# Eight later attention units: transposing in VectorE blocks of 32 and a ScalarE exchange in place of TensorE transposes

## The chip, the cores and the metric

The kernel runs on one core of one Trainium2 chip. The time is the device time of one execution in microseconds (us); lower is better. The kernel before took 783.46 us as the median of three runs (781.99 to 783.51). Engines are named as the profile names them: PE is TensorE, DVE is VectorE, ACT is ScalarE, POOL is GpSimd, SP issues most DMAs.

## The reference

Chunked attention is followed by a gated two-layer product. q, k and v have 8 batches, 8 heads, 576 positions and 64 dimensions; positions attend only within chunks of 64.

```
scores = scale * q_c @ k_c.T              # 64 x 64 for each batch, head and chunk
attn = exp(scores - rowmax) / (rowsum + 1e-9)
x = (attn @ v_c) laid out as 4608 x 512
h = x @ w_in                              # 512 x 2048
g = h * clip(h + 3, 0, 6) / 6
out = g @ w_out                           # 2048 x 512
```

All is float32. The kernel writes the output transposed.

## The kernel before

The 4608 tokens are nine blocks of 512. Each block has two attention units (`n`, `dp`), named "50" for block 5, first half; a unit covers four heads of the block's eight chunks, so 32 score squares of 64 x 64, which fill 128 partitions and two PSUM banks. There are 18 units. Block 0 is multiplied plainly, and the blocks 1 to 8 are taken in four pairs by a scheme of seven block products in place of eight; pair s has a first product (steps `f1` to `f7` for eight parts p) and a second (steps `s{s}.0` to `s{s}.55`). A step is six PE matmuls of 128 x 512: three passes (L354 to L356), since each operand is split into a high and a low part. The splitting is ACT's and DVE's work (L541, L544, L983, L987). Between the two products stand the sums of the scheme (L876), the relu (L761, ACT) and the gate (L764, DVE). In a first product the sums read and free PSUM banks that later steps of the same product need: `u2` and `u4` (L876, DVE, tiles u<-h,p and u<-acc,u), then the third sum (h<-acc,u), the relu, the gate.

An attention unit goes through these steps: `scores` (PE, L246) into the two-bank PSUM tile `two`; `max` (DVE, L253); `less` (DVE, L257), which subtracts the row maximum and writes the SBUF tile `e`; `exp` (ACT, L260); `sum` (DVE, L264 to L266); `share` (DVE, L284), which multiplies by the reciprocal sum; `turn` (PE, L296), eight transposes of 128 x 128 against the identity into a new `two`; `turned` (ACT, L300), which copies the transposed tile back over `e`; `product` with v (PE, L322), which in most units has the next unit's `scores` behind it as one step; and `keep` (ACT, L335). Units in the list `ROWS` ("30", "31", "40", "41") replace less, exp and sum: `negate` (DVE, L270) makes the bias, 16 exponentials of 128 x 64 with row sums (ACT, L276, two to a step) read `two` and write `e`, and `invert` (DVE, L280 and L281) ends it.

The order on every engine is made before the program is written: `Schedule.order` plays all steps through with the costs that stand in the code (1.07 us for `turn`, 1.15 us for two row exponentials and so on), due times and a fixed list of dependences, and each engine's queue gets its instructions in the order that comes out. An engine runs its queue in order, so a wait holds up all that is behind it.

The units "50" to "81" are the later ones: the order is 50, 60, 61, 51 in the stage of the second pair and 70, 80, 81, 71 in that of the third. 50, 60, 70 and 80 are prepared mostly beside a first product, the other four beside a second.

Of the kernel before, what the change touches and what calls it, by code (L numbers as in the profile page):

```python
# [9 lines left out]
F32 = mybir.dt.float32  # L10
# [8 lines left out]
P = 128  # L19
CH = 64  # L20
B, H, S, D = 8, 8, 576, 64
NDP = H // 4
NB = 8
NT = NB * CH
# [13 lines left out]
ORDER_B = (1, 5, 6, 7, 2, 4, 3)  # L38
SLOTS = 7 * NFP
HALF = [slice(0, CH), slice(CH, P)]  # L40
WARM = 12
FILL = (2.0, 4.0)
LAG = 2
ROWS = ["30", "31", "40", "41"]
XDVE = ["x0.s0c", "x0.s2", "x0.s2b", "x0.s3", "x0.s3b"]
SHARED = 0.6
OVERLAP = {"DVE": 0.07, "ACT": 0.0}
# [15 lines left out]
STEPS = SECOND - PART * 7 * (NFP - NPL)  # L63
COMBS = []
LATE = (5, 9)


class Schedule:
# [69 lines left out]
def tile_kernel(ctx: ExitStack, tc: tile.TileContext, qk_in, v_in, weights, out):  # L138
    nc = tc.nc
    PE, ACT, DVE, POOL = nc.tensor, nc.scalar, nc.vector, nc.gpsimd  # L140
# [3 lines left out]
    ap = pool("ap", 1)  # L144
# [78 lines left out]
    class Attention:  # L223


        def __init__(self, n, dp, psum=None, out=None):
            self.n, self.dp = n, dp
            self.psum = psum or (lambda: two_banks(ps_a))
            self.out = out or self.psum

        def load_qk(self, qk=None):

# [7 lines left out]

        def scores(self):
            self.s = self.psum().rearrange("p a (c t) -> p a c t", t=CH)
            for c in range(NB):
                for a, rows in enumerate(HALF):
                    for o in HALF:
                        PE.matmul(self.s[o, a, c, :], lhsT=self.qk[rows, 0, c, o], rhs=self.qk[rows, 1, c, o], start=True, stop=True)  # L246
# [6 lines left out]
            DVE.tensor_reduce(out=self.m, in_=self.flat(self.s), axis=AX.X, op=ALU.max)  # L253

        def lessen(self, e=None):
            self.e = e if e is not None else ap.tile([P, 2, NB, CH], F32, name="e")
            DVE.tensor_tensor(out=self.flat(self.e), in0=self.flat(self.s), in1=self.wide(self.m), op=ALU.subtract)  # L257

        def exp(self):
# [11 lines left out]

        def exps(self, k, e=None):
            if k == 0:
                self.e = e if e is not None else ap.tile([P, 2, NB, CH], F32, name="e")
            for c in range(2 * k, 2 * k + 2):
                ACT.activation(out=self.flat(self.e)[:, c], in_=self.flat(self.s)[:, c], func=AF.Exp, bias=self.m[:, c:c + 1], scale=SCALE,  # L276
                               accum_out=self.z[:, c:c + 1])
# [20 lines left out]
        def turned(self, part=(0, 1)):  # L298
            of = slice(part[0], part[-1] + 1)
            ACT.copy(out=self.aT[:, of], in_=self.tp[:, of])  # L300

        def transpose(self):
            self.turn()
# [324 lines left out]
    def attention(u, due, scores=(), less=(), keep=(), bank=None):  # L628
        n, dp = int(u[0]), int(u[1])
        a = heads[u]  # L630
# [4 lines left out]
            heads[after].scores()  # L635

        e = spare.get("e" + u, lambda: None)
        rows = [("less", "DVE", 1.23, lambda: a.lessen(e()), less), ("exp", "ACT", 1.06, a.exp, ()), ("sum", "DVE", 1.68, a.total, ())]
        if u in ROWS:
            rows = [("negate", "DVE", 0.12, a.negate, ()), *[(f"exp{k}_", "ACT", 1.15, lambda k=k: a.exps(k, e() if k == 0 else None), less if k == 0 else ()) for k in range(8)],  # L640
                    ("invert", "DVE", 0.45, a.invert, ())]
        steps = [("scores", "PE", 1.30, a.scores, ["qk" + u, *scores]), ("max", "DVE", 1.23, a.largest, ()), *rows, ("share", "DVE", 1.22, a.share, ()), ("turn", "PE", 1.07, a.turn, ()),
                 ("turned", "ACT", 1.02, a.turned, ()), ("product", "PE", 2.26 if after else 1.50, products if after else a.product,
                  ["v" + u, *(["qk" + after, *[x for _ in HALF for x in work.take(*RINGS[bank], "product" + u, [made[u], *alike.get(u, [])])]] if after else [])]),
                 ("keep", "ACT", 1.24 if after else 1.03, a.keep, keep)]
        if n == 0:
# [184 lines left out]
    def swap():  # L831
        nonlocal op, tp
        std.close()
        op = pool("op2", 2)
        tp = pool("tp", 2)
# [294 lines left out]
```

## Time and profile before

| what | value |
| --- | --- |
| median of three runs | 783.46 us |
| profiled execution, device time | 782.89 us |
| its span (first to last instruction) | 781.1 us |
| PE busy | 772.8 us, 99% |
| DVE busy | 644.8 us, 83% |
| ACT busy | 398.2 us, 51% |
| POOL busy | 70.7 us, 9% |
| PE share of the chain that ended last | 94% |
| granted TensorE clock | 0.999 |

The chain that ended last is followed back from the last instruction; what stands on it set the end. Busy shares are averages over stages with different limits. A PE matmul's shown duration is longer than the time until the next can start, since matmuls are pipelined.

### The profile page before, as it was taken

The numbers are of one execution on the slowest core, as the hardware profiler recorded it, in microseconds if no ns is written. First come the engines' busy times: TensorE is split into PE (matmuls) and PEld (weight loads), VectorE is DVE, ScalarE is ACT, GpSimd is POOL, SyncE is SP. The second block draws the span as 40 slices with busy tenths as digits, with TensorE's granted clock in tenths as the row PEclk, the third lists the DMA queues.
The fourth block names the chain that finished last, engine by engine and source line by source line (L and its number), as shares of the span: only waits on it lengthen the run. The fifth ranks groups of instructions, "written<-read, shape, count | busy, mean of one in ns | idle before, by whom it ended". The sixth has DMA issues, their size and how long they took to land.

```text
span 781.1 us, 14021 instructions
## 1 busy us (share of the span) xinstructions
PE 772.8 (99%) x5604; PEld 635.3 (81%) x5604; DVE 644.8 (83%) x808; ACT 398.2 (51%) x593; POOL 70.7 (9%) x55
## 2 busy tenths in 40 slices
PE   8999999999999999999999999999999999999998
PEld 4788888887888888888888878888888888888887
DVE  6999999999999999867998677678997657679741
ACT  4999843566667744344744434436644333355330
POOL 0000000000000001323200003231100013222000
PEclk9999999999999999999999999999999999999999
DMA  9999999878869997566667685667557665566572
GB/s 371 405 402 328 341 350 308 297 242 251 265 214 337 345 349 246 192 215 229 220 236 256 223 283 189 217 227 242 204 193 222 216 204 194 197 210 202 194 238 90
DMA packets 69426, 198.06 MB, mean 254 GB/s; under 512 B 7024, under 2 KB 19568, under 8 KB 65008
## 3 DMA queue, kind: packets, MB, share of 16 engines
q1 hardware_dynamic: 69216, 197.03, 73.7%
q8 instruction: 44, 0.72, 0.4%
q14 instruction: 22, 0.18, 0.1%
q10 hardware_dynamic: 144, 0.13, 0.0%
HBM read 153.09 MB, written 44.04 MB: 252 GB/s over the span
## 4 chain that ended last, share of the span: by engine, by line
PE 94%; DVE 3%; DMA 1%; issue 0%; SPq 0%; ACT 0%; DVEq 0%; ACTq 0%
PE acc L354 21%; PE acc L355 21%; PE acc L356 21%; PE h L354 8%; PE h L356 8%; PE h L355 8%; PE two L246 2%; PE two L296 2%; PE h L322 2%; DMA out_t<-u 1%; DMA b<-hl 1%; PE h L172 1%; PE two L322 1%; DVE wb L764 0%; PE h L370 0%
## 5 line engine op out<-in xcount | busy, mean ns | idle before, releaser
L354 PE MATMUL acc<-wa,ws 128*128 128x512 f32 (+1 forms) x536 | 209.4, 391 | 0.3 <-DVE u L876 0.3
L356 PE MATMUL acc<-wa,ws 128*128 128x512 f32 (+1 forms) x536 | 207.8, 388 | 0.0
L355 PE MATMUL acc<-wa,ws 128*128 128x512 f32 (+1 forms) x536 | 207.8, 388 | 0.0
L983 ACT CAST wa<-wb 128x1024 fp32r<-128x1024 f32 x96 | 100.4, 1052 | 93.4 <-PE acc L356 53.6
L987 DVE TENSOR_TENSOR wa<-wb,wa 128x1024 fp32r<-128x1024 f32 x96 | 122.6, 1289 | 21.3 <-ACT wa L983 21.2
L354 PEld LDWEIGHTS acc<-wa,ws 128*128 128x128 f32 x536 | 100.7, 188 | 21.7 <-DVE u L876 0.8
L356 PEld LDWEIGHTS acc<-wa,ws 128*128 128x128 f32 x536 | 100.6, 188 | 20.7
L355 PEld LDWEIGHTS acc<-wa,ws 128*128 128x128 f32 x536 | 100.7, 188 | 19.9
L950 POOL TENSOR_TENSOR wb<-wb 128x512 f32<-128x512 f32 x24 | 32.9, 1372 | 634.6 <-DVE wb L764 321.4
L761 ACT ACTIVATE r<-acc,half 128x512 f32<-128x512 f32 x90 | 61.3, 687 | 42.3 <-DVE acc L876 37.5
L761 ACT ACTIVATE r<-h,half 128x512 f32<-128x512 f32 x38 | 26.2, 689 | 103.0 <-DVE h L876 95.8
L764 DVE SCALAR_TENSOR_TENSOR wb<-r,acc 128x512 f32<-128x512 f32 x90 | 60.8, 681 | 5.3 <-ACT r L761 5.0
L355 PE MATMUL h<-wa,ws 128*128 128x512 f32 (+1 forms) x144 | 55.2, 383 | 0.0
L356 PE MATMUL h<-wa,ws 128*128 128x512 f32 (+1 forms) x144 | 55.2, 383 | 0.0
L354 PE MATMUL h<-wa,ws 128*128 128x512 f32 (+1 forms) x144 | 55.2, 383 | 0.0
L876 DVE TENSOR_TENSOR u<-h,p 128x512 f32<-128x512 f32 x32 | 21.9, 686 | 30.1 <-PE h L356 24.5
L876 DVE TENSOR_TENSOR acc<-acc,u 128x512 f32<-128x512 f32 x48 | 33.0, 695 | 8.6 <-PE acc L356 8.5
L952 POOL TENSOR_TENSOR g<-wb,wb 128x512 f32<-128x512 f32 x24 | 37.0, 1542 | 1.9
L764 DVE SCALAR_TENSOR_TENSOR wb<-r,h 128x512 f32<-128x512 f32 x38 | 25.8, 679 | 11.6 <-ACT r L761 11.6
L354 PE MATMUL acc<-wa,wa 128*128 128x512 f32 x88 | 34.9, 396 | 0.0
L355 PE MATMUL acc<-wa,wa 128*128 128x512 f32 x88 | 34.3, 390 | 0.0
L356 PE MATMUL acc<-wa,wa 128*128 128x512 f32 x88 | 34.3, 390 | 0.0
(199 smaller groups left out, 1391.8 us busy)
## 6 DMA issues: line engine op xcount, KB each, us to landing
ws<-b SPq DMA_DIRECT2D x84, 512.0 KB, 4.6
ws<-a SPq DMA_DIRECT2D x72, 512.0 KB, 4.5
qk<-qk_in SPq DMA_DIRECT2D x17, 1024.0 KB, 7.8
wa<-b SPq DMA_DIRECT2D x28, 512.0 KB, 6.2
a<-wa SPq DMA_DIRECT2D x40, 256.0 KB, 6.0
v<-v_in SPq DMA_DIRECT2D x17, 512.0 KB, 5.7
wa<-w_in_out SPq DMA_DIRECT2D x8, 1024.0 KB, 12.5
wb<-w_in_out SPq DMA_DIRECT2D x8, 1024.0 KB, 10.9
```

Source lines behind the costliest of these rows:

```text
L246: PE.matmul(self.s[o, a, c, :], lhsT=self.qk[rows, 0, c, o], rhs=self.qk[rows, 1, c, o], start=True, stop=True)
L322: PE.matmul(po[s][o, a, i, :], lhsT=self.v[rows, a, i, o], rhs=self.aT[rows, a, i, o], start=True, stop=True)
L354: PE.matmul(ps, lhsT=a_h, rhs=b_h, start=first, stop=False, skip_group_check=more)
L355: PE.matmul(ps, lhsT=a_h, rhs=b_l, start=False, stop=False, skip_group_check=more)
L356: PE.matmul(ps, lhsT=a_l, rhs=b_h, start=False, stop=last, skip_group_check=more)
L761: ACT.activation(out=t["r"], in_=ps(), func=AF.Relu, bias=half, scale=1.0 / 6.0)
L764: work.add("gate" + name, "DVE", 0.69, ["relu" + name, *more], lambda: DVE.scalar_tensor_tensor(out=out(), in0=t["r"], scalar=1.0, in1=ps( ...
L876: return lambda: DVE.tensor_tensor(out=out(), in0=x(), in1=y(), op=ALU.add)
L950: work.add(id_("t1."), "POOL", 1.45, [id_("gate3."), id_("gate2.")], lambda f=gq: POOL.tensor_tensor(out=f(0, 1), in0=f(0, 1), in1=f(0, 0) ...
L952: work.add(id_("t2."), "POOL", 1.45, [id_("t1."), id_("gate7.")], lambda f=gq, p=p: POOL.tensor_tensor(out=t2_of(p), in0=f(1, 1), in1=f(0, ...
L983: ACT.copy(out=g_ops[s, i, pp][:, :, 0], in_=src())
L987: work.add(low, *(("POOL", 2.5) if on else ("DVE", 1.22)), [high], lambda i=i, pp=pp, src=src, on=POOL if on else DVE: on.tensor_tensor(ou ...
```

## The change

For the units 50, 51, 60, 61, 70, 71, 80 and 81 (`FLIPPED`) the PE transposes and the ACT copy after them go. In their place DVE transposes the whole tile from PSUM into SBUF in blocks of 32 x 32 (`flip`), and ACT puts the blocks in their places in three steps of five copies (`swap`): `save` copies half of the blocks into the first bank of the unit's score tile in PSUM, `down` moves blocks between partition quarters in SBUF (two copies of 32 partitions), `up` moves the saved ones back (two copies). So that this exchange gives the wanted layout, `scores` writes the 64 x 64 squares to other places. Softmax of these units is done in place in PSUM: `less`, `exp`, `sum` and `share` read and write `two` instead of `e`, and `e` is first written by `flip`. Four of the units (60, 61, 80, 81) join `ROWS`; their 16 row exponentials read and write `two` in place. The planner's cost of a pair of row exponentials goes from 1.15 to 0.62 us for all units that have them, and `flip`, `save`, `down` and `up` get costs of their own.

```diff
-ROWS = ["30", "31", "40", "41"]
+ROWS = ["30", "31", "40", "41", "60", "61", "80", "81"]
+FLIPPED = ("50", "51", "60", "61", "70", "71", "80", "81")
...
         def scores(self):
             self.s = self.psum().rearrange("p a (c t) -> p a c t", t=CH)
+            if self.flipped:
+                for i in range(NB // 2):
+                    for k, o in enumerate(HALF):
+                        for a, rows in enumerate(HALF):
+                            for s, to in enumerate(HALF):
+                                PE.matmul(self.s[to, a, 2 * i + k, :], lhsT=self.qk[rows, 0, 2 * i + s, o], rhs=self.qk[rows, 1, 2 * i + s, o], start=True, stop=True)
+                return
...
-            self.e = e if e is not None else ap.tile([P, 2, NB, CH], F32, name="e")
+            self.e = self.s if self.flipped else e if e is not None else ap.tile([P, 2, NB, CH], F32, name="e")
...
+        def flip(self):
+            t = ap.tile([P, 2 * NB * CH], F32, name="e")
+            DVE.transpose(out=t, in_=self.e.rearrange("p a c t -> p (a c t)"))
+            self.aT = t.rearrange("p (a i t) -> p a i t", a=2, t=P)
+            blocks = t.rearrange("p (n h t) -> p n h t", h=2, t=CH // 2)
+            spare_ = self.e.rearrange("p a c t -> p (a c t)")[:, :NT].rearrange("p (n t) -> p n t", t=CH // 2)
+            self.moves = [[(spare_, blocks[:, :, 0])],
+                          [(blocks[hi, :, 0], blocks[lo, :, 1]) for lo, hi in QUARTER],
+                          [(blocks[lo, :, 1], spare_[hi]) for lo, hi in QUARTER]]
+
+        def swap(self, k):
+            for to, of in self.moves[k]:
+                ACT.copy(out=to, in_=of)
...
-        rows = [("less", "DVE", 1.23, lambda: a.lessen(e()), less), ("exp", "ACT", 1.06, a.exp, ()), ("sum", "DVE", 1.68, a.total, ())]
+        rows = [("less", "DVE", 1.23, lambda: a.lessen(e()), () if u in FLIPPED else less), ("exp", "ACT", 1.06, a.exp, ()), ("sum", "DVE", 1.68, a.total, ())]
         if u in ROWS:
-            rows = [("negate", "DVE", 0.12, a.negate, ()), *[(f"exp{k}_", "ACT", 1.15, lambda k=k: a.exps(k, e() if k == 0 else None), less if k == 0 else ()) for k in range(8)],
+            rows = [("negate", "DVE", 0.12, a.negate, ()), *[(f"exp{k}_", "ACT", 0.62, lambda k=k: a.exps(k, e() if k == 0 else None), less if k == 0 and u not in FLIPPED else ()) for k in range(8)],
                     ("invert", "DVE", 0.45, a.invert, ())]
-        steps = [("scores", "PE", 1.30, a.scores, ["qk" + u, *scores]), ("max", "DVE", 1.23, a.largest, ()), *rows, ("share", "DVE", 1.22, a.share, ()), ("turn", "PE", 1.07, a.turn, ()),
-                 ("turned", "ACT", 1.02, a.turned, ()), ("product", "PE", 2.26 if after else 1.50, products if after else a.product,
+        steps = [("scores", "PE", 1.30, a.scores, ["qk" + u, *scores]), ("max", "DVE", 1.23, a.largest, ()), *rows, ("share", "DVE", 1.22, a.share, ()), *([("flip", "DVE", 1.22, a.flip, less), ("save", "ACT", 0.56, lambda: a.swap(0), ()), ("down", "ACT", 1.0, lambda: a.swap(1), ()), ("up", "ACT", 1.0, lambda: a.swap(2), ())]
+                   if u in FLIPPED else [("turn", "PE", 1.07, a.turn, ()), ("turned", "ACT", 1.02, a.turned, ())]), ("product", "PE", 2.26 if after else 1.50, products if after else a.product,
```

On PE, in the first product beside which unit 50 is prepared; `wa` is a step's left operand, and lines are numbered as in each kernel (L354 before is L378 after). Before:

```order
L354 MATMUL acc<-wa_3334,ws 128x512
L355 MATMUL acc<-wa_3334,ws 128x512
L356 MATMUL acc<-wa_3334,ws 128x512
L296 MATMUL two<-ident,e 128x128 x8
L354 MATMUL acc<-wa_3346,ws 128x512
L355 MATMUL acc<-wa_3346,ws 128x512
L356 MATMUL acc<-wa_3346,ws 128x512
```

After:

```order
L378 MATMUL acc<-wa_3333,ws 128x512
L379 MATMUL acc<-wa_3333,ws 128x512
L380 MATMUL acc<-wa_3333,ws 128x512
L378 MATMUL acc<-wa_3345,ws 128x512
L379 MATMUL acc<-wa_3345,ws 128x512
L380 MATMUL acc<-wa_3345,ws 128x512
```

The eight transposes between two steps are gone, and the steps follow each other directly; this happens at eight places.

On ACT, from unit 70's `keep` (L335 before, L359 after) on, where unit 80's exponentials stand among the relus (L761, L785) and the copies to `p` (L934, L958) of a first product. Before:

```order
L335 COPY xa<-h 128x8x64 x2
L260 ACTIVATE e<-e 128x1024
L761 ACTIVATE r<-h,half 128x512
L761 ACTIVATE r<-acc,half 128x512 x3
L934 COPY p_5379<-acc 128x512
L761 ACTIVATE r<-h,half 128x512
L761 ACTIVATE r<-acc,half 128x512 x3
L934 COPY p_5458<-acc 128x512
```

After:

```order
L359 COPY xa<-h 128x8x64 x2
L286 ACTIVATE two,z<-two,m 128x64 x10
L785 ACTIVATE r<-h,half 128x512
L785 ACTIVATE r<-acc,half 128x512
L286 ACTIVATE two,z<-two,m 128x64 x4
L785 ACTIVATE r<-acc,half 128x512
L286 ACTIVATE two,z<-two,m 128x64 x2
L785 ACTIVATE r<-acc,half 128x512
L958 COPY p_5401<-acc 128x512
L785 ACTIVATE r<-h,half 128x512
L785 ACTIVATE r<-acc,half 128x512
L324 COPY two<-e 128x512
```

One exponential of the whole tile has become 16 of 64 columns, ten of them ahead of the round's first relu, four ahead of the third and two ahead of the fourth; `save` (L324) stands ahead of the next round's third relu. The three steps of the exchange are ended eight ACT rows ahead of the `keep` that follows unit 80's product. Each of the 16 exponentials but the first waits in the program for ACT's own one before it, which those of the units 30 to 41 don't do.

On DVE in the same round, from the first two gates (L764 before, L788 after) on. Before:

```order
L764 SCALAR_TENSOR_TENSOR wb_2060<-r,h 128x512
L764 SCALAR_TENSOR_TENSOR wb_2135<-r,acc 128x512
L876 TENSOR_TENSOR acc<-acc,u_5317 128x512 x2
L764 SCALAR_TENSOR_TENSOR wb_2135<-r,acc 128x512
L764 SCALAR_TENSOR_TENSOR wb_2060<-r,acc 128x512
L284 TENSOR_TENSOR e<-e,z 128x1024
L876 TENSOR_TENSOR u_5401<-h,p_5379 128x512
L876 TENSOR_TENSOR u_5403<-acc,u_5401 128x512
L876 TENSOR_TENSOR h<-acc,u_5403 128x512
L764 SCALAR_TENSOR_TENSOR wb_2060<-r,h 128x512
```

After:

```order
L788 SCALAR_TENSOR_TENSOR wb_2135<-r,acc 128x512
L900 TENSOR_TENSOR acc<-acc,u_5328 128x512 x2
L788 SCALAR_TENSOR_TENSOR wb_2135<-r,acc 128x512
L290 TENSOR_SCALAR z<-z 128x16
L291 RECIPROCAL z<-z 128x16
L788 SCALAR_TENSOR_TENSOR wb_2060<-r,acc 128x512
L294 TENSOR_TENSOR two<-two,z 128x1024
L900 TENSOR_TENSOR u_5422<-h,p_5401 128x512
L900 TENSOR_TENSOR u_5424<-acc,u_5422 128x512
L900 TENSOR_TENSOR h<-acc,u_5424 128x512
L314 STREAM_TRANSPOSE e<-two 128x1024
L788 SCALAR_TENSOR_TENSOR wb_2060<-r,h 128x512
```

The subtraction and the reduction of the whole tile, which stood ahead of these rows, are gone; `share` (L284, L294) now stands behind the fourth gate and works in PSUM, and the block transpose (L314) stands between the next round's third sum and its first gate.

## Rows read from the trace of the kernel before

**Rows 1.** The page, part 1: busy time, share of the span and instructions of each engine.
```profile
PE 772.8 (99%) x5604; PEld 635.3 (81%) x5604; DVE 644.8 (83%) x808; ACT 398.2 (51%) x593; POOL 70.7 (9%) x55
```

**Rows 2.** Busy time by stretch: each engine's busy us in three stretches, then clock and DMA.
```profile
200.00:300.00 100.00, 100.00 (x810) 83.11 (x809) 98.03 (x125) 65.75 (x154) 0.00 (x0) 1.00 0.87 300
380.00:420.00 40.00, 40.00 (x422) 33.37 (x421) 38.12 (x36) 20.74 (x23) 2.41 (x2) 1.00 0.63 214
540.00:580.00 40.00, 40.00 (x300) 33.21 (x300) 38.73 (x41) 24.11 (x28) 2.60 (x2) 1.00 0.64 212
```

**Rows 3.** Timeline of PE around unit 50's transposes: start us, us, what.
```profile
339.89 0.39 PE L356 MATMUL acc<-wa,ws 128*128 128x512 f32 x1
340.12 1.03 PE L296 MATMUL two<-ident,e 128*128 128x128 f32 x8
340.91 0.48 PE L354 MATMUL acc<-wa,ws 128*128 128x512 f32 x1
341.22 0.40 PE L355 MATMUL acc<-wa,ws 128*128 128x512 f32 x1
```

**Rows 4.** Groups by line, PE from 300 us: busy us, mean ns, idle before.
```profile
L296 PE MATMUL two<-ident,e 128*128 128x128 f32 x64 | 8.3, 272 | 0.0
```

**Rows 5.** Groups by line, DVE from 300 to 620 us, softmax lines.
```profile
L264 DVE TENSOR_REDUCE z<-e 128x16 f32<-128x1024 f32 x8 | 9.7, 1211 | 1.2 <-ACT e L260 1.2
...
L257 DVE TENSOR_TENSOR e<-two,m 128x1024 f32<-128x1024 f32 x7 | 8.5, 1221 | 0.1
L253 DVE TENSOR_REDUCE m<-two 128x16 f32<-128x1024 f32 x7 | 8.5, 1217 | 2.4 <-PE two L246 2.4
...
L265 DVE TENSOR_SCALAR z<-z 128x16 f32<-128x16 f32 x8 | 1.9, 240 | 0.3
```

**Rows 6.** Groups by line, ACT from 300 to 620 us.
```profile
L934 ACT COPY p<-acc 128x512 f32<-128x512 f32 x15 | 8.7, 579 | 3.0 <-PE acc L356 3.0
L260 ACT ACTIVATE e<-e 128x1024 f32<-128x1024 f32 x8 | 8.5, 1060 | 9.0 <-DVE e L257 9.0
...
L300 ACT COPY e<-two 128x1024 f32<-128x1024 f32 x8 | 8.1, 1016 | 2.7 <-PE two L296 2.5
```

**Rows 7.** Timeline of ACT in a unit that takes exponentials by rows.
```profile
259.06 0.32 ACT L276 ACTIVATE e<-two,m 128x64 f32<-128x64 f32 x1 [1.51 <-DVE m L270]
259.27 0.20 ACT L276 ACTIVATION_READ_ACCUMULATOR e<-two,m 128x1 f32 x1
259.37 0.31 ACT L276 ACTIVATE e<-two,m 128x64 f32<-128x64 f32 x1
```

**Rows 8.** Timeline of ACT in the first product of unit 80's stage.
```profile
502.39 1.07 ACT L335 COPY xa<-h 128x512 f32<-128x512 f32 x2 [0.49 <-PE h L322]
...
508.63 0.69 ACT L761 ACTIVATE r<-h,half 128x512 f32<-128x512 f32 x1 [1.63 <-DVE h L876]
509.22 0.68 ACT L761 ACTIVATE r<-acc,half 128x512 f32<-128x512 f32 x1
512.05 1.29 ACT L761 ACTIVATE r<-acc,half 128x512 f32<-128x512 f32 x2 [2.15 <-DVE acc L876]
```

**Rows 9.** Timeline of DVE in the same stretch.
```profile
503.36 1.23 DVE L253 TENSOR_REDUCE m<-two 128x16 f32<-128x1024 f32 x1 [1.21 <-PE two L246]
504.62 1.22 DVE L257 TENSOR_TENSOR e<-two,m 128x1024 f32<-128x1024 f32 x1
...
512.77 1.28 DVE L764 SCALAR_TENSOR_TENSOR wb<-r,acc 128x512 f32<-128x512 f32 x2 [0.22 <-ACT r L761]
513.98 1.94 DVE L284 TENSOR_TENSOR e<-e,z 128x1024 f32<-128x1024 f32 x1
...
516.59 0.69 DVE L876 TENSOR_TENSOR u<-acc,u 128x512 f32<-128x512 f32 x1
...
518.91 0.69 DVE L764 SCALAR_TENSOR_TENSOR wb<-r,h 128x512 f32<-128x512 f32 x1 [0.82 <-ACT r L761]
```

**Rows 10.** Timeline of PE's weight loads there.
```profile
518.10 0.19 PEld L354 LDWEIGHTS acc<-wa,ws 128*128 128x128 f32 x1
```

More of the change, by code (lines that the diff above doesn't have):

```diff
@@ L40 @@
 HALF = [slice(0, CH), slice(CH, P)]
+QUARTER = [(slice(0, 32), slice(32, 64)), (slice(64, 96), slice(96, 128))]
 WARM = 12
@@ L229, in __init__ @@
             self.out = out or self.psum
+            self.flipped = f"{n}{dp}" in FLIPPED
         def load_qk(self, qk=None):
@@ L273, in exps @@
             if k == 0:
-                self.e = e if e is not None else ap.tile([P, 2, NB, CH], F32, name="e")
+                self.e = self.s if self.flipped else e if e is not None else ap.tile([P, 2, NB, CH], F32, name="e")
             for c in range(2 * k, 2 * k + 2):
```

## The prediction

> **What bounds the kernel now.** I read the page's busy shares first. PE works 99% of the span with 772.8 us, DVE 83%, ACT 51% [rows 1]; the reader is to see that only PE has no room on the average. Next the busy time by stretch: in all three stretches shown PE is busy for the whole stretch, at clock 1.00, also in the two late ones where DVE is fullest (38.12 and 38.73 of 40 us) [rows 2]. So in the part where the change works every step of PE lies on the path that sets the end, and the other engines count only where they would make PE wait. Last I went to the place of one `turn`, to see what it takes from PE, and to the round of a first product where PE is nearest to waiting.
>
> **What leaves PE.** Around unit 50's `turn` PE starts a matmul at 339.89, the transposes at 340.12 and the next matmul at 340.91 [rows 3]: 340.91 - 340.12 = 0.79 us for eight transposes. The matmul behind them starts its follower after 341.22 - 340.91 = 0.31 us, where the usual distance is 0.23 us (340.12 - 339.89), so 0.08 us more go in the switch. One `turn` takes 0.87 us; there are 64 transposes from 300 us on, hence eight units [rows 4], and 8 x 0.87 = 7.0 us leave PE. The mean duration of 272 ns in that row isn't used, since transposes overlap. `scores` and `product` keep their number and shapes of matmuls; I cost their new places at nothing.
>
> **What DVE gets and loses.** Four units lose `less` and the reduction of `sum`, 4 x (1.22 + 1.21) = 9.7 us [rows 5], and get a `negate`, which I put at 0.2 us after L265, the mean of a small operation on 16 columns [rows 5]. All eight get a block transpose of 128 x 1024 from PSUM, which no row of before shows. The nearest row is the reduction L253, which reads the same tile from PSUM in 1.22 us [rows 5]; upwards the slowest operation on a tile of that size is a `share` of 1.94 us [rows 9]; below the reduction's time a faster one would give PE nothing. I take 1.22, since the reduction too reads each element once from PSUM: 8 x 1.22 = 9.8 us. The sum is 9.8 + 0.8 - 9.7 = +0.9 us on DVE, over stretches that it fills to 95 and 97% at most, and in those two a unit by rows (61, 81) gives back 2.4 - 0.2 - 1.2 = 1.0 us. PE's 40 us shrink there by two `turn`s to 38.3, DVE's 38.12 and 38.73 to 37.1 and 37.7: it still fits. The softmax in place in PSUM I cost at nothing: the reductions from PSUM and from SBUF take 1217 and 1211 ns [rows 5]. At 1.94 us the transpose would come 0.7 us later, inside the 0.82 us that PE has to spare there, worked out below.
>
> In the Trainium skill, "VectorE: DVE Perf Modes", section "The three transpose paths", a 128 x 128 bf16 block takes VectorE 311 ns; no run here shows it. Eight such blocks would be an estimate of 2.49 us by that page, twice the reduction; what it would do is the second rival.
>
> **What ACT gets.** `turned` (1.02 us [rows 6]) becomes five copies of 512 columns, bounded by the 0.58 us of a 128 x 512 copy [rows 6] on one side and twice that on the other (pieces of 32 columns, 32 partitions); I take 0.58, as the columns are the same: 2.9 us, +1.9 a unit. The order gives the exchange time: it is over eight ACT rows ahead of the `keep` behind unit 80's product, so PE doesn't wait for `up`; what stands behind `save` on ACT is the round's third relu.
>
> The row exponentials are the larger item. In before a pair starts 259.37 - 259.06 = 0.31 us apart, because the second begins ahead of the end of the first's accumulator read (259.27 + 0.20 = 259.47) [rows 7]. In the new units each waits for the one before, as the order says. How ACT takes such a wait no row shows. On DVE, `less` waits for `max` and starts 504.62 - 504.59 = 0.03 us after its end [rows 9]. So the distance becomes 259.47 + 0.03 - 259.06 = 0.44 us; the bounds are 0.31 (the wait costs nothing) and 0.32 + 0.20 + 0.03 = 0.55 us (nothing overlaps). I take 0.44, because reads and activations of one exponential overlapped in every pair. A unit by rows then takes ACT 16 x 0.44 = 7.0 us in place of 1.06 [rows 6].
>
> **What lies behind that wait.** I walk unit 80 on the clock of before, since there (and for 60, which stands in the same round of the earlier stage) the exponentials stand among the relus of a first product, by whose sums PE gets its banks back. `keep` ends at 503.46 [rows 8], `max` at 504.59; with `negate` the exponentials start at 504.85. Ten take until 509.25, where the first relu stood at 508.63: 0.62 late. Two relus at a distance of 0.59 us (509.22 - 508.63), then four exponentials, end at 510.43 + 1.76 = 512.19, where the third relu stood at 512.05. It, two exponentials and the fourth relu end at 512.19 + 0.59 + 0.88 + 0.69 = 514.35. On DVE `invert` waits for the last exponential, and behind it stand the fourth gate and `share`: gate until 515.0, share until 516.2 (at 1.22) or 517.0 (at 1.94), where it ended at 515.92 [rows 9]. So `u2` and `u4` of the next round come 0.3 to 1.0 us later. Before, `u4` ended at 517.28 [rows 9] and PE's load that needs its bank began at 518.10 [rows 10]: 0.82 us spare. PE waits 0 to 0.2 us; I take 0.1 for each of the two, 0.2 us in all. At a distance of 0.31 us the ten would end at 507.95, ahead of the relu, and PE waits nowhere. At 0.55 the same walk gives 510.35, 511.53, 513.73, 516.11, 516.8 and 518.0 to 518.7: 2.1 to 2.8 late, less 0.82 is 1.3 to 2.0 us a unit, 2.6 to 4.0 us for both. For 61 and 81, beside a second product, ACT works further ahead of PE; there I take nothing.
>
> The planner's new 0.62 us also moves steps of the units 30 to 41. PE is busy for all of 200 to 300 us [rows 2], its work there stays, so nothing, give or take 0.5 us. No DMA is added, dropped or moved on SP.
>
> **The sum.** -7.0 + 0.2 = -6.8 us against the profiled execution's 782.89 us (span 781.1 and 1.8 around it) gives 776.1. The median of before is 0.57 above that execution, so I say 776.7 us.
>
> **Rivals.**
>
> First: the waits between row exponentials cost what the upper bound says. For it: nothing in before shows ACT waiting for itself. Against: the reads overlapped in rows 7. Then 776.7 - 0.2 + 2.6 to 4.0 = 779.1 to 780.5 us.
>
> Second: the block transpose takes about 2.5 us. In unit 80's round it stands between the third sum and the first gate, where DVE waited 0.82 us [rows 9]. It would come 1.27 us later than forecast, less 0.82 is 0.45 us of PE's time in each of the four units beside a first product, 1.8 us: 778.5 us. Against it: full-tile operations of DVE take 1.21 to 1.94 us.
>
> Third: all of the shown duration of the transposes comes back. The row gives 272 ns each [rows 4], 64 x 0.272 = 17.4 us, so 783.46 - 17.4 = 766.1 us. Against it: eight starts lie within 0.79 us. In the Trainium skill "TensorE: Matmul & The Clock Gate", Part 4, PE-mode transpose, gives about 275 ns for one in a kernel's context; the trace agrees on the duration, not on the time that the next has to wait.
>
> Fourth: the exchange's copies take twice the row, 1.16 us each. The five would then take 5.8 us in a round of 7 steps x 6 matmuls x 0.23 = 9.7 us, and what stands behind them on ACT would come 2.9 us later than forecast; less 0.82 that is 2.1 us in each of the four units beside a first product, 8.4 us, and the gain is gone: 783.46 - 7.0 + 8.4 = 784.9 us, or 780.7 where ACT's idle time takes up half. For it: no row has copies of 32 partitions with short pieces.
>
> Fifth, slower: the block transpose is far slower, and DVE becomes the engine that PE waits for. The idle times of DVE in the rows of unit 80's round are 1.21 + 0.22 + 0.82 = 2.2 us [rows 9]; what a transpose takes above 1.2 + 2.2 = 3.4 us PE pays in each of the four units beside a first product. From 3.4 + 7.0 / 4 = 5.2 us on the gain is gone; at 6 us the time is 783.46 - 7.0 + 4 x 2.6 = 786.9 us. Four times the reduction speaks against it.
>
> **How the numbers follow.** Forecast 0.64 (its own range 775.0 to 777.9: the runs of before lie 1.5 below to 0.1 above their median, and 61, 81 or the early units may cost up to a microsecond), first rival 0.17, second 0.08, third 0.02, fourth 0.06, fifth 0.03. The range from 774.8 to 780.3 us holds the forecast, the second and most of the first. This kernel's measurement can't tell less than 0.2%, 1.6 us, from no change. Faster by more: the first three cases and the third rival, and a little of the fourth, 0.91; within: 0.06; slower by more: the fifth, 0.03.
>
> **What would show it.** Right: no L296 row after 300 us; PE busy for the whole of the later stretches; the sum of PE's busy time about 7 us lower; STREAM_TRANSPOSE near 1.2 us; row exponentials of the new units 0.44 us apart; the load behind `u4` in the rounds of 60 and 80 starting close behind it. Wrong: gaps on PE behind DVE's u<-acc,u in those two rounds (first rival), behind the block transpose in four (second), or behind `up`.

## The result, and the profile after

The changed kernel takes 776.52 us, the kernel before 783.18 us beside it (medians of six runs). One run of each lies far above its others; without it the medians are 776.15 and 782.91 us, and the ratio is 0.9912, 95% interval 0.9896 to 0.9928. The prediction was 776.7 us. The profiled execution took 776.96 us, its span is 775.1. The page's busy times and the three stretches of [rows 1, 2] now read:

```profile
PE 766.4 (99%) x5538; PEld 628.8 (81%) x5540; DVE 644.4 (83%) x812; ACT 432.3 (56%) x749; POOL 70.6 (9%) x55
```

```profile
200.00:300.00 100.00, 100.00 (x809) 83.11 (x808) 97.65 (x125) 64.63 (x154) 0.00 (x0) 1.00 0.88 304
380.00:420.00 40.00, 40.00 (x414) 33.16 (x413) 37.82 (x37) 26.36 (x57) 2.94 (x2) 1.00 0.67 226
540.00:580.00 40.00, 40.00 (x296) 33.17 (x295) 38.13 (x40) 27.97 (x58) 4.37 (x2) 1.00 0.63 206
```

PE lost 6.4 us of busy time and still has no idle time in the three stretches: it is the bound as before. DVE's sum is 0.4 us lower, ACT's 34 us higher. The groups by line that answer to [rows 4 to 6], from the whole execution; the number behind the bar is the busy time, then the mean ns:

```profile
L314 DVE STREAM_TRANSPOSE e<-two 128x1024 f32<-128x1024 f32 x8 | 9.9, 1242 | 0.0
L294 DVE TENSOR_TENSOR two<-two,z 128x1024 f32<-128x1024 f32 x8 | 9.8, 1227 | 0.1
```

```profile
L286 ACT ACTIVATE two<-two,m 128x64 f32<-128x64 f32 x64 | 18.4, 288 | 5.0 <-PE acc L380 2.8 <-DVE m L280 0.5
...
L324 ACT COPY e<-e 32x512 f32<-32x512 f32 x16 | 9.9, 618 | 0.4
L324 ACT COPY e<-two 32x512 f32<-32x512 f32 x16 | 9.3, 580 | 0.4
...
L324 ACT COPY two<-e 128x512 f32<-128x512 f32 x8 | 4.7, 591 | 4.0 <-DVE e L314 4.0
```

The block transpose takes 1.24 us and a copy of the exchange 0.58 to 0.62, also the copies of 32 partitions. The view of the transposes' line (after a duration's minimum, median and maximum it gives the first and the last start) shows that the last one on PE starts at 275.0 us:

```profile
L306 PE MATMUL two<-ident,e x72: 270/272/299, 15.2 to 275.0; 128*128 128x128 f32 x72
```

**Where the time went.** Both kernels load the same 3120 weights of 128 x 128 into PE for the products (the transposes' left out). I take the start of the n-th such load in each trace and subtract; between two places where PE does the same work, the difference moves only by what PE won or lost. For the last load it is 771.18 - 777.14 = -5.96 us:

| from | after minus before, change in us | what |
| --- | --- | --- |
| first load (21 us) | +0.47 | start of the program |
| 173 to 182 | +0.89 | PE waits for DVE in the first pair's first product |
| 338 to 608 | 8 x -0.89 | eight places, one for each `turn` |
| 465 to 471 | -0.21 | a stall that both kernels have is shorter |

So the mechanism is the one forecast, and 0.89 us a `turn` stands beside the 0.87 that [rows 3] gave. The two positive lines have nothing to do with the changed units; they are what kept this execution at -6.0 in place of -7.4 us. The first lies between -0.2 and +0.5 us in the other executions; the experiments tell what the second is.

### The profile page after: what moved, and what is told of

Its sections match the earlier page's. It is cut to its first block, busy times and chain, and to the rows that moved or that the text cites. A ratio compares the mean times of both kernels' runs of the same rounds, so it can differ in the third digit from the quotient of the medians.

```text
span 775.1 us, 14046 instructions
## 1 busy us (share of the span) xinstructions
PE 766.4 (99%) x5538; PEld 628.8 (81%) x5540; DVE 644.4 (83%) x812; ACT 432.3 (56%) x749; POOL 70.6 (9%) x55
## 4 chain that ended last, share of the span: by engine, by line
PE 93%; DVE 3%; DMA 2%; ACT 1%; issue 1%; SPq 0%; DVEq 0%; ACTq 0%
PE acc L378 21%; PE acc L379 21%; PE acc L380 21%; PE h L378 8%; PE h L380 8%; PE h L379 8%; PE h L346 2%; PE two L256 1%; PE two L251 1%; PE two L306 1%; DMA b<-hl 1%; DMA out_t<-u 1%; PE h L174 1%; PE two L346 1%; PE h L394 0%
## 5 line engine op out<-in xcount | busy, mean ns | idle before, releaser
L378 PE MATMUL acc<-wa,ws 128*128 128x512 f32 (+1 forms) x536 | 208.8, 390 | 0.1
L1011 DVE TENSOR_TENSOR wa<-wb,wa 128x1024 fp32r<-128x1024 f32 x96 | 120.3, 1271 | 17.7 <-ACT wa L1007 17.5
L378 PEld LDWEIGHTS acc<-wa,ws 128*128 128x128 f32 x536 | 100.7, 188 | 21.7 <-DVE u L900 0.5
L785 ACT ACTIVATE r<-acc,half 128x512 f32<-128x512 f32 x90 | 61.5, 686 | 31.2 <-DVE acc L900 26.8
L785 ACT ACTIVATE r<-h,half 128x512 f32<-128x512 f32 x38 | 26.1, 687 | 91.2 <-DVE h L900 83.9
L788 DVE SCALAR_TENSOR_TENSOR wb<-r,acc 128x512 f32<-128x512 f32 x90 | 61.1, 683 | 6.7 <-ACT r L785 6.2
L378 PE MATMUL h<-wa,ws 128*128 128x512 f32 (+1 forms) x144 | 55.2, 383 | 0.0
L788 DVE SCALAR_TENSOR_TENSOR wb<-r,h 128x512 f32<-128x512 f32 x38 | 25.9, 681 | 11.8 <-ACT r L785 11.8
L378 PE MATMUL acc<-wa,wa 128*128 128x512 f32 x88 | 34.9, 397 | 0.2 <-DVE h L900 0.2
```

The lines of the kernel that those rows point to most:

```text
L378: PE.matmul(ps, lhsT=a_h, rhs=b_h, start=first, stop=False, skip_group_check=more)
L785: ACT.activation(out=t["r"], in_=ps(), func=AF.Relu, bias=half, scale=1.0 / 6.0)
L788: work.add("gate" + name, "DVE", 0.69, ["relu" + name, *more], lambda: DVE.scalar_tensor_tensor(out=out(), in0=t["r"], scalar=1.0, in1=ps( ...
L1011: work.add(low, *(("POOL", 2.5) if on else ("DVE", 1.22)), [high], lambda i=i, pp=pp, src=src, on=POOL if on else DVE: on.tensor_tensor(ou ...
```

## The experiments

Unless a time is named, numbers are of the one profiled execution, compared load by load as above.

**The early units' planner cost put back.**

```diff
-(f"exp{k}_", "ACT", 0.62, ...
+(f"exp{k}_", "ACT", 0.62 if u in FLIPPED else 1.15, ...
```

> The changed kernel, but the planner's cost of a pair of row exponentials is 0.62 us only for the eight changed units; the early units 30 to 41 are planned with 1.15 us as before. In the profile of the changed kernel PE loses some 0.9 us against the kernel before between 167 and 193 us, with three short stalls at 175 to 179 us, before any changed unit. Theory A: that loss comes from the early units' steps being put in another order by the new cost. Then the loss is gone, the pace up to 330 us is that of before within 0.5 us, and the time is about 775.6 us (0.9 below the changed kernel's 776.5). Rival B: the loss is from one execution to the next or belongs to the start of the program; then the pace shows it again or the time stays at 776.5 us within 0.4.

776.4 us (775.04 to 777.09; ratio 0.9912, 0.9898 to 0.9925). Between 173 and 182 us PE lost 0.25 us in place of 0.89, as theory A said; the time that it forecast (775.6) didn't come. In the profiled execution the stall at 465 us grew by 0.60 us against before, which takes that gain back; for the other three executions this isn't shown.

**All eight flipped, but no new units by rows.** `ROWS` as before.

> The changed kernel with all eight units transposed by VectorE, but units 60, 61, 80 and 81 keep less, exp and sum on VectorE and ScalarE in one piece, as before. VectorE gets 4 x (1.22 + 1.21 - 0.17) = 9.0 us more than in the changed kernel. Theory A: VectorE still has the room for the block transpose, since it idles 2 us or more in each 40 us; the eight turns are all that counts: 776.3 us (776.0 to 777.0). Rival B: in the stretches beside a second product, where VectorE was 37.8 and 38.1 of 40 us in the changed kernel, another 2.3 us in a unit leave no room, and PE waits 0.5 to 1 us a unit: 777.5 to 779 us, with gaps on PE behind VectorE.

776.39 us (775.94 to 776.92): theory A. DVE does 651.2 us in place of 644.4, 6.8 us more where 9.0 was expected, and the two full stretches take it:

```profile
380.00:420.00 40.00, 40.00 (x414) 33.16 (x413) 39.09 (x37) 21.75 (x26) 2.48 (x2) 1.00 0.69 228
540.00:580.00 40.00, 40.00 (x296) 33.16 (x295) 38.71 (x41) 23.35 (x28) 3.51 (x2) 1.00 0.63 207
```

PE is busy for all of both, and past 330 us it loses nothing against the changed kernel but 0.47 us at 465. So the row exponentials, which took most of the prediction's walk, bought nothing here.

**The row exponentials alone.** `FLIPPED = ()`, `ROWS` with the four new units.

> The other half alone: the list of units by rows has 60, 61, 80 and 81 too, with the planner's new cost, but no unit is transposed by VectorE; all eight turns stay on PE, and the exponentials write the SBUF tile. VectorE has 4 x 2.3 = 9 us less to do. Theory A: only the turns on PE set the time: as before within 0.6 us, 783.2 us (and up to 0.9 us more if the new planner cost for the early units is a loss). Rival B: part of the gain came from the relief of VectorE: 780 to 782 us.

783.8 us (782.79 to 785.39; ratio 1.001, 1.0001 to 1.0019): theory A. The gain belongs to the turns. This run has the changed kernel's early order, yet PE loses nothing at 173 to 183 us. The DVE rows say why. First the changed kernel, then this one:

```profile
162.42 1.80 DVE L482 TENSOR_TENSOR a<-a 128x256 f32<-128x256 f32 x4 [0.91 <-DMA a<-wa]
...
172.74 1.21 DVE L294 TENSOR_TENSOR e<-e,z 128x1024 f32<-128x1024 f32 x1
173.87 0.68 DVE L900 TENSOR_TENSOR g<-h,g 128x512 f32<-128x512 f32 x1
```

```profile
161.61 1.80 DVE L482 TENSOR_TENSOR a<-a 128x256 f32<-128x256 f32 x4
...
171.92 1.21 DVE L294 TENSOR_TENSOR e<-e,z 128x1024 f32<-128x1024 f32 x1
173.05 0.68 DVE L900 TENSOR_TENSOR g<-h,g 128x512 f32<-128x512 f32 x1
```

In the first DVE waits 0.91 us for a transfer, in the second not at all, and all that follows is 0.8 us later or earlier, up to a sum for which PE waits in the changed kernel:

```profile
175.80 0.19 PEld L378 LDWEIGHTS acc<-xd,hl 128*128 128x128 f32 x1 [0.42 <-DVE g L900]
```

With the old cost put back, the first place reads:

```profile
172.01 0.68 DVE L900 TENSOR_TENSOR g<-h,g 128x512 f32<-128x512 f32 x1
172.61 1.22 DVE L294 TENSOR_TENSOR e<-e,z 128x1024 f32<-128x1024 f32 x1
```

The sum stands ahead of `share` there, which leaves room for a late transfer. So both expectations held a part: the order takes the room, the execution decides how much of it is missed. (The late transfer isn't all of it: in the run with doubled copies DVE waits for none there, and PE loses 0.47 us.)

**Half of it: 70, 71, 80, 81 alone.** Both lists cut to these (by rows: 80, 81).

> Only the four units 70, 71, 80 and 81 are transposed by VectorE, and only 80 and 81 join the units by rows; 50 to 61 are as before. Theory A: every turn removed is worth 0.87 us of PE, whatever stage it stands in: 4 x 0.87 = 3.5 us below before, 779.7 us (779.3 to 780.6). Rival B: the stages are not alike, and one of them gives nearly all or nearly nothing: 777.5 or 782.

780.07 us (779.13 to 780.7; ratio 0.9959, 0.9946 to 0.9971): four steps of 0.89 us at the four places, none at the others. Theory A.

**The block transpose twice.** The `DVE.transpose` line stands twice in `flip`.

> The changed kernel, with each block transpose run twice, the second right behind the first: 2.48 us of VectorE in place of 1.24 in each of the eight units, in the same order on every engine. Rival two of the prediction priced just this: 0.45 us of PE's time in each of the four units beside a first product, 1.8 us in all, so a span 1.8 us above the changed kernel's 775.1. Theory A, from the changed kernel's trace: in those rounds PE waits for the sum u4, and u4 starts only after PE's own matmul before it, 0.8 us ahead of the load that needs it, however late VectorE was before; a transpose 1.24 us longer is taken up by VectorE's idle time, and the loss is 0 to 0.5 us in all, what there is of it in the stretches beside a second product, where VectorE is 37.8 and 38.1 of 40 us.

Span 775.4. PE loses 0.18 us at 331 us, in unit 50's round, where its load waits for u4:

```profile
330.68 0.69 DVE L901 TENSOR_TENSOR u<-acc,u 128x512 f32<-128x512 f32 x1
331.43 0.19 PEld L379 LDWEIGHTS acc<-wa,ws 128*128 128x128 f32 x1 [0.31 <-DVE u L901]
```

It loses 0.31 us at 469 us, in unit 70's round, behind the gate; another 0.24 at 465 us is the store's stall, and beside the second products it loses less than 0.1 us. So theory A has the size, some 0.5 us in all, but not the place, which is rival two's: two of its four units pay 0.2 to 0.3 us in place of 0.45, and DVE's idle time takes the rest.

**The block transpose five times.** The same line five times.

> The changed kernel, with each block transpose run five times in a row: 6.2 us of VectorE in each of the eight units. The prediction's fifth rival: what goes above 3.4 us is paid by PE in the four units beside a first product, (6.2 - 3.4) x 4 = 11.2 us, so a span of about 786. Theory B: VectorE's idle time of two units (some 2.2 us in 40 us beside a second product, where two units take 9.9 us more) is what counts, and the four units beside a second product pay more than the four beside a first one: 14 to 25 us, a span of 789 to 800, most of it in the stretches 380 to 420 and 540 to 580 us.

Span 804.1, a loss of 29.2 us, more than either expected; and it is not where theory B put it: 22.3 us in the four rounds beside a first product, 7.0 beside a second. The windows around unit 50's round (PE, PEld, DVE, ACT, POOL, then PE's granted clock as a share of 2.4 GHz) show a part that neither had:

```profile
316.00:321.00 5.00, 5.00 (x24) 4.14 (x23) 4.43 (x6) 1.85 (x4) 2.59 (x2) 1.00 0.73 244
321.00:325.00 4.00, 1.26 (x6) 0.72 (x4) 3.92 (x4) 0.56 (x1) 0.00 (x0) 0.97 0.33 99
325.00:327.00 2.00, 1.24 (x3) 1.04 (x4) 1.88 (x3) 1.89 (x5) 0.00 (x0) 0.50 0.00 0
327.00:329.00 2.00, 2.00 (x6) 1.52 (x6) 1.37 (x3) 1.79 (x3) 0.00 (x0) 0.50 0.00 0
329.00:331.00 2.00, 2.00 (x6) 1.57 (x5) 1.17 (x2) 0.69 (x1) 0.00 (x0) 0.50 0.59 168
331.00:333.00 2.00, 2.00 (x9) 1.58 (x8) 1.48 (x3) 0.80 (x2) 0.34 (x1) 0.85 0.51 178
```

No matmul started between 321.87 and 325.76; PE then ran at the lower level, 1.2 GHz, into the window from 331 to 333 us, with a matmul every 0.43 us in place of 0.23. The round loses 6.5 us, of which the stall itself is 3.7 (325.76 - 321.87 less 0.23).

**The exchange's copies twice.** Each `ACT.copy` of `swap` is issued twice.

> The changed kernel, with each of the five copies of the exchange run twice: some 6.1 us of ScalarE in a unit in place of 3.05. Rival four of the prediction: what stands behind them on ScalarE comes 2.9 us later than forecast, less 0.82 is 2.1 us of PE's time in each of the four units beside a first product: a span 8.4 us above 775.1, or 4.2 where ScalarE's idle time takes up half. Theory A: ScalarE is busy for 26 to 29 of 40 us at most, its idle times stand between the relus of the same rounds, and the gates have over 1.2 us before PE needs their banks: 0 to 1 us in all.

Span 781.3: a loss of 6.7 us in the flipped units' rounds, 5.1 beside the first products and 1.6 beside the second. (PE also loses 0.84 us at 276 to 279 us, ahead of the first block transpose, for which no cause is shown; 1.3 us less at the start, at 174 and at 465 us make the span's growth 6.2.) Theory A was wrong: ACT's idle time on the average was no cover. Unit 50's round on ACT, and the load that waits behind it:

```profile
320.82 2.55 ACT L325 COPY e<-e 32x512 f32<-32x512 f32 x4
323.38 2.40 ACT L325 COPY e<-two 32x512 f32<-32x512 f32 x4
325.81 0.69 ACT L786 ACTIVATE r<-h,half 128x512 f32<-128x512 f32 x1
```

```profile
327.87 0.19 PEld L379 LDWEIGHTS acc<-wa,ws 128*128 128x128 f32 x1 [1.70 <-DVE wb L789]
```

The relu, whose inputs were ready, stood behind the copies on ACT's queue; the gate waited for it, and PE for the gate's bank. In the changed kernel that relu started at 322.80 and PE didn't wait.

**Exponentials not in place.** `exps` writes the SBUF tile `e`, `share` writes back to `two`.

> The changed kernel, but the row exponentials of 60, 61, 80 and 81 read the PSUM tile and write the SBUF tile, as in the early units, and share reads the SBUF tile and writes the product back to PSUM for the transpose. So no exponential waits for the one before it; the order on the engines stays. The prediction: the distance of two exponentials falls from 0.44 to 0.31 us, and PE gains 0.2 us in all (0.1 in each of the rounds of 60 and 80). Theory A, from the changed kernel's trace, which shows no stall of PE in those rounds: the distance falls to 0.31 us and PE gains nothing, the span stays as in the changed kernel but for the start. Rival B: the distance stays 0.44, since the accumulator reads and not the wait set it.

The distance falls from 0.44 to 0.30 us. First the changed kernel, then this one:

```profile
501.60 0.29 ACT L286 ACTIVATE two<-two,m 128x64 f32<-128x64 f32 x1 [1.42 <-PE acc L380]
501.82 0.19 ACT L286 ACTIVATION_READ_ACCUMULATOR two<-two,m 128x1 f32 x1
502.04 0.29 ACT L286 ACTIVATE two<-two,m 128x64 f32<-128x64 f32 x1
```

```profile
502.24 0.31 ACT L286 ACTIVATE e<-two,m 128x64 f32<-128x64 f32 x1 [1.42 <-PE acc L383]
502.45 0.19 ACT L286 ACTIVATION_READ_ACCUMULATOR e<-two,m 128x1 f32 x1
502.55 0.31 ACT L286 ACTIVATE e<-two,m 128x64 f32<-128x64 f32 x1
```

In the rounds of 60 and 80 the pace stays within 0.05 us: theory A. In the changed kernel an exponential starts 0.03 us after the accumulator read before it has ended (501.82 + 0.19), as the prediction worked it out; the edit takes 0.14 us off the distance, and PE pays nothing for it. It also moves the output from PSUM to SBUF; that the wait alone makes the difference wasn't tested. (The span is 775.8; the stall at 465 us is 0.57 longer.)

**Two more units, 40 and 41.** Both join `FLIPPED`.

> The changed kernel, with units 40 and 41, which are prepared beside the second product of the first pair (215 to 300 us), transposed by VectorE too: ten units in place of eight. Theory A: every turn that leaves PE is worth 0.89 us: 1.8 us below the changed kernel by the pace of PE's weight loads, span about 773.3. Rival B: in that stretch VectorE is busy for 97.65 of 100 us in the changed kernel, and both units are by rows already, so nothing is taken off it: 97.65 + 2 x 1.24 = 100.1 us of work meet a PE that needs 100 - 1.8 = 98.2 us; PE waits for VectorE for 1.9 us or more, and the gain is gone or turned: span 775 to 777, with stalls between 215 and 310 us.

Span 778.8: rival B's outcome, dearer than its bound, but not from a full DVE alone. The same edit puts these units' exponentials in place, at the slower distance, and gives them the exchange. So DVE's `invert` waited for the last exponential in both units, and unit 40's product for the exchange's last copy, which takes back what its `turn` gave:

```profile
244.73 0.17 DVE L290 TENSOR_SCALAR z<-z 128x16 f32<-128x16 f32 x1 [0.94 <-ACT two L286]
271.62 0.17 DVE L290 TENSOR_SCALAR z<-z 128x16 f32<-128x16 f32 x1 [0.59 <-ACT two L286]
```

```profile
252.31 0.19 PEld L346 LDWEIGHTS h<-e,v 64*64 64x64 f32 x4 [0.86 <-ACT e L324]
```

From unit 41's `invert` on, DVE, and PE's load behind it:

```profile
274.20 1.22 DVE L490 TENSOR_TENSOR hl<-a,hl 128x1024 fp32r<-128x1024 f32 x1
275.33 1.24 DVE L314 STREAM_TRANSPOSE e<-two 128x1024 f32<-128x1024 f32 x1
276.50 1.18 DVE L1011 TENSOR_TENSOR wa<-wb,wa 128x1024 fp32r<-128x1024 f32 x1
```

```profile
277.74 0.19 PEld L379 LDWEIGHTS acc<-wa,wa 128*128 128x128 f32 x1 [3.25 <-DVE wa L1011]
```

The operand's low half (L1011) stands behind the transpose on a DVE that has no gap left there; PE waits 3.25 us, and its clock is 0.50 in the window from 280 to 282 us. From 271 to 285 us PE falls 4.2 us behind the kernel before, though unit 41's `turn` is gone. What share of it the transpose has and what the late `invert`, no run separates.

**The last output sums in their own tile.**

```diff
-send(row(r, e), col(c), of(k, e), of(y, e), i == 7, ...
+send(row(r, e), col(c), of(k, e), of(y, e), i in (7, 3), ...
```

> The changed kernel, but the last output sums of a second product (o3) are written into a tile of their own kind instead of the tile of u4, as those of o7 are. In the runs so far the first u4 of the third pair's first product (about 465 us) waits for the store of that tile to land, and PE waits behind it: two starts of PE are 0.73 us apart there before, 0.52 in the changed kernel, 1.33 and 0.98 in two of the variants, where 0.23 is usual. Theory A: the stall goes in full: 0.3 us against the changed kernel's profile, and up to 1.1 against the variants. Rival B: the tile's own ring, or the sum u2 ahead of u4, waits next, and the stall stays.

The stall at 465 us is gone in full. The row of u4 in the run with the early cost, and in this one:

```profile
463.72 0.69 DVE L900 TENSOR_TENSOR u<-acc,u 128x512 f32<-128x512 f32 x1 [2.13 <-DMA out_t<-u]
```

```profile
462.25 0.69 DVE L900 TENSOR_TENSOR u<-acc,u 128x512 f32<-128x512 f32 x1
```

The store no longer holds the tile: in the twelve executions traced without this edit this u4 waits 0.32 to 2.13 us for it, in the two with it not at all. PE wins 0.42 us there against the changed kernel. But in five of the twelve, with waits up to 0.96 us, PE didn't stall either, so theory A's gain in time isn't shown by this one execution.

**The changed kernel once more, and both edits together**, the tile for o3 and the early cost, on one chip.

> The changed kernel once more, beside the version below, on the same chip and against the same runs of before: 776.5 us (775 to 777.3), 0.87 to 0.88% below before.

> The changed kernel with the two edits of earlier runs together: the output sums o3 get a tile of their own, and the early units 30 to 41 are planned with 1.15 us for a pair of row exponentials as before. Theory A: both places where PE still stalls by a transfer that lands late are eased: 0.3 to 0.6 us at 465 us and on average some 0.6 us at 173 to 183 us (there the pace of eight runs with the new cost is 0 to 1.15 us behind that of before, the one run with the old cost is 0.25 behind): 775.5 us, 0.5 to 1.2 us below the changed kernel beside it. Rival B: the place at 173 to 183 us depends on the execution and not on the order, and only the first edit counts: 776.1 us, which these runs can't tell from the changed kernel.

776.24 us (775.66 to 776.8; ratio 0.9911, 0.9897 to 0.9924) and 775.05 us (774.95 to 776.0; ratio 0.9897, 0.9884 to 0.9911). The medians are 1.2 us apart, the lowest three of four runs of the version lie below all five of the other; the two intervals overlap. Load by load the version loses 0.18 us at 173 to 182 and gains 0.63 at 465 us, the changed kernel loses 0.82 and gains 0.55. So in this pair of traces theory A's saving is there at the first place (0.64 us) and hardly at the second (0.08); the version is most likely the faster of the two. At 173 to 183 us eleven executions with the new early cost stand 0 to 1.15 us behind before, ten of them 0.47 or more; the two with the old cost 0.18 and 0.25.

## Why the prediction was right, step by step

- **What leaves PE.** 0.89 us a turn for 0.87, eight times, at eight places: 7.15 us for 7.0. Distances between starts gave it; the duration of 272 ns (third rival) would have given 17.4. Half the units gave half, the row exponentials alone nothing.
- **The block transpose.** 1.24 us for 1.22. The reduction from the same PSUM tile was the right row. Run twice, 2.48 us, it cost PE some 0.5 us in all, so the second rival's price of 1.8 us was too high as well. The estimate of 2.49 us worked out from the Trainium skill, "VectorE: DVE Perf Modes", section "The three transpose paths", does not agree with the trace: L314 shows half of that for fp32 in blocks of 32.
- **DVE's sum.** Forecast +0.9 us, measured 644.4 - 644.8 = -0.4. The failed term is `share`, which I had left at its duration: in before two of eight took 1.94 us (one is in [rows 9]), now none is above 1.23, which makes up 1.4 us. See the last section.
- **ACT's copies.** Five took 0.59 + 1.26 + 1.18 = 3.03 us in unit 50's round, for 2.9. The fourth rival's mechanism is real: doubled, they cost 5.1 us beside the first products, between its 8.4 and the 4.2 with half taken up, and 1.6 beside the second, which it lacked. What spoke against it was the duration alone, not the room on ACT.
- **The row exponentials.** The distance of 0.44 us was measured to the hundredth, with a first exponential at 501.60, which is 504.88 on the clock of before for a forecast of 504.85. The first rival's 0.55 us, and its price with it, didn't come.
- **What lies behind them.** This term failed, by its size: +0.2 us was forecast (0.1 for each of two rounds, between 0 for a `share` of 1.22 us and 0.2 for one of 1.94), 0 measured. Unit 80's round after, on PE, DVE and then PE's load (add 3.28 us for the clock of before):

```profile
512.09 0.39 PE L380 MATMUL h<-wa,ws 128*128 128x512 f32 x1
```

```profile
511.24 1.23 DVE L294 TENSOR_TENSOR two<-two,z 128x1024 f32<-128x1024 f32 x1
512.59 0.69 DVE L900 TENSOR_TENSOR u<-h,p 128x512 f32<-128x512 f32 x1
513.31 0.69 DVE L900 TENSOR_TENSOR u<-acc,u 128x512 f32<-128x512 f32 x1
514.11 0.70 DVE L900 TENSOR_TENSOR h<-acc,u 128x512 f32<-128x512 f32 x1
514.72 1.24 DVE L314 STREAM_TRANSPOSE e<-two 128x1024 f32<-128x1024 f32 x1
```

```profile
514.81 0.19 PEld L378 LDWEIGHTS acc<-wa,ws 128*128 128x128 f32 x1
```

`share` took 1.23 us and ends at 512.47, 0.45 us ahead of the forecast (516.2 - 3.28 = 512.92): the walk counted 0.44 us behind every exponential, but the relu behind the last of a group starts 0.30 us after it, three times in the round:

```profile
505.54 0.29 ACT L286 ACTIVATE two<-two,m 128x64 f32<-128x64 f32 x1
505.84 0.68 ACT L785 ACTIVATE r<-h,half 128x512 f32<-128x512 f32 x1
```

u2 (u<-h,p) starts 0.11 us after the end of PE's last matmul into its bank (512.09 + 0.39); on the clock of before that is 515.87, where it stood there too. So PE sets it, not `share`, and u4 ends at 514.00, which is 517.28 before: not a hundredth later than in [rows 9]. The 0.82 us from u4's end to PE's load was rightly read as room: in the run with the transpose twice the load that waits starts 0.05 us or so behind u4's end (330.68 + 0.69 and 331.43), so nearly all of the 0.81 us seen here was still to spare.
- **The early units.** "Nothing, give or take 0.5" was too narrow: the new planner cost moves `share` ahead of a sum, and PE lost 0.89 us there. The profiled execution's net, -6.0 us, is thus 0.8 short of the sum of -6.8, and the medians (-6.7 here, -7.1 in the repeat) lie on both sides of it. That the median came within 0.2 us of the forecast is partly luck: the turns gave 0.15 us more than forecast and the walk's 0.2 us wasn't paid, and in the traced execution a start 0.5 us later and the 0.9 us at 173 to 182 us, neither in the sum, worked against that.
- **The fifth rival** had its place right (the four units beside a first product) and its price too low: at 6.2 us it gives 11.2 us, the trace 22.3 there and 7.0 beside the second products, which it lacked. It lacked the lower clock behind the stalls, too.

## What to carry to other kernels

What an instruction on the bounding engine is worth is the distance of its start to the next one's, and it comes back in full only while the engine that takes over the work is not late itself: the same edit gave 0.89 us a unit in the later stages, where VectorE had gaps, and for the units 40 and 41 cost 3.7 us of span, where VectorE waited for ScalarE first and then had no gap left. Room is read, in queue order, from the idle time ahead of the instruction that another engine waits for and from the distance between its end and the other's start; an engine that is idle for a third of a stretch can still be late in one round of it, as the doubled copies showed. And with a change of 0.9% it is worth comparing executions load by load: at two places where a transfer can land late, neither part of the changed units, an execution won or lost up to about as much as one unit gave.

## What the runs showed of the hardware that was not expected

- Two shares of before ran beside POOL's sums and took 1.94 us, as in [rows 9], where POOL's own L952 took 2.16 us. The share in PSUM ran beside POOL too and took 1.23, and POOL kept its 1.29. Here the share from 511.24 to 512.47, with

```profile
511.47 1.29 POOL L976 TENSOR_TENSOR g<-wb,wb 128x512 f32<-128x512 f32 x1
```

  So in this kernel the two slowed each other where VectorE's tile was in SBUF, and not where it was in PSUM. In the run with exponentials not in place, `share` reads SBUF and writes PSUM; there the two beside POOL (at 358.39 and 511.20) took 1.62 us and POOL's L979 2.16, so they were slowed without writing to SBUF. That the place of what is read is the cause fits all of these; no run was made for it.
- The five longest waits of PE's loads past 200 us, one of 3.25 us with the units 40 and 41 and four of 3.46 to 4.26 us with the transpose five times, were each followed by the lower clock, 0.50, for some 3 to 7 us. Waits of 2.23 and 2.35 us in the latter run were not; in the run with doubled copies the load waited 1.70 us and the clock was 1.00 in the window from 326 to 330 us.
- A copy of 32 partitions x 512 elements on ScalarE took 0.58 to 0.62 us, as long as one of 128 x 512 (0.59).
- An exponential that waits for the one before on ScalarE, in place in PSUM, starts 0.44 us after it; one that doesn't, writing to SBUF, 0.30 us.
